# Dense block of a two-layer transformer: second weights fetched slot by slot during the projection, split rows made anew instead of kept in DRAM, the fourth block's rows turned in two parts

## The chip, the core and the metric

The kernel runs on one core of a Trainium2 chip. Its engines work from queues of their own: TensorE (PE in the profile, PEld its weight loads), VectorE (DVE), ScalarE (ACT), GpSimd (POOL) and SyncE (SP), which here issues nearly all transfers. The metric is the time of one execution on the device in microseconds; the median of the runs is compared. It was measured at 3495.49 us before the change.

## What is computed

Two equal layers, each an attention block and a dense block with a residual addition around it, on 2048 rows of 640 numbers (float32):

```python
def _A_ref(x, wqkv, wo):                     # 32 heads of 20
    q, k, v = split(x @ wqkv)
    scores = jnp.einsum("bhqd,bhkd->bhqk", q, k) * (Dh ** -0.5)
    p = _softmax(scores, axis=-1)
    o = jnp.einsum("bhqk,bhkd->bhqd", p, v)
    return heads_side_by_side(o) @ wo
def _B_ref(x, w1, b1, w2, b2):               # 640 -> 1536 -> 640
    h = relu(x @ w1 + b1)
    return (h * h) @ w2 + b2
x = x + _A_ref(_layernorm(x), A_wqkv, A_wo)  # layer one
x = x + _B_ref(_layernorm(x), B_w1, B_b1, B_w2, B_b2)
x = x + _A_ref(_layernorm(x), A_wqkv, A_wo)  # layer two
x = x + _B_ref(_layernorm(x), B_w1, B_b1, B_w2, B_b2)
```

## The kernel before

**Numbers in two halves.** A float32 matrix is held as a high and a low part (a cast to float32r by ACT, and the difference by DVE), and each product is three matmuls (high x high, high x low, low x high). A *split row tile* `xnT` is [128, 2, 512]: 128 of the 640 features, both parts, 512 rows of the sequence; five of them (`KD = 5`) hold one block of rows.

**Blocks.** The sequence is cut into four blocks of 512 rows (`NQB = 4`). After a layer's attention comes the *projection* (`add_heads`): for each block, four tiles of 128 rows, each in two halves of 320 columns, 15 matmuls per half at L361; DVE adds the residual from the PSUM bank (L1355) and the result goes to DRAM (`d_x`). After each half, 8 times a block, `side()` runs one step of other work: steps 0 to 23 of `plan` belong to the second, third and fourth quarter of the projection (8 to a quarter).

**Turning the rows.** The dense block needs normalised rows with the features on the partitions. `turn_out` does it for a block in six steps: statistics (L312, L313), normalisation (L320) and a 32 x 32 transposition on DVE (L1383) for each of four tiles, each then written to DRAM in `d_t` by four transfers of 128-byte pieces. `turn_in` reads the block back as five tiles of 256 KB, and in five more steps casts (ACT, L1398) and subtracts (DVE, L1399): the split rows.

**The dense block** (`mlp`) goes over the first half of the 1536 hidden features (`fh = 0`) for the four blocks, then over the second (`fh = 1`). For one half and one block PE makes six chains of 15 products of 512 columns (L361, by `w_1`), ACT applies relu and square (L1449, L1450), DVE and ACT form sums of the halves, and 126 products of 320 columns (L1475, by `w_2`, seven products in place of eight) follow in 14 *parts* (the first 36 products open the sums, six parts have 3 more, eight have 9). Behind each part DVE adds a PSUM bank to a row tile (L1494; in some parts also the bias, L1496). A `side()` call stands before the block (-1), after each of the six chains (0 to 5), after them (6), and after each part (7 to 20). `put(gen, ...)` names the sides at which the next steps of a generator run.

**Where things lie.** 41 slots of 512 KB (`arena`) hold weights, split rows and operands of the dense block; 12 tiles of 320 KB (`xp`) hold row tiles `x`, turned tiles `y` and hidden rows `r`. The first weights `w_1` are 15 slots (8 for the first half), the second weights `w_2` 14 slots of 480 KB for each half. A slot that is taken again waits for its last reader. PSUM has eight banks, used in turn.

**Order.** Nothing is rescheduled: each engine runs its instructions in the order in which the program's text emits them, SP's transfers too. A transfer on SP whose data or slot isn't ready holds up all behind it. Before the change all of `w_1`'s first 8 slots and 3 of `w_2` are fetched after the projection's first quarter, then 5, 4 and the last 2 after the second, the third and the fourth (`loads`). Each block's split rows are written to DRAM (`d_xn`) during the first half's block, and read back by `again` for the second half. The fourth block's rows are turned out in the first dense block, at sides -1, -1, 0, 2, 4, 5. Layer one also turns its results for the next layer's attention in the second half (`ahead`): blocks three and four of `fh = 1` read them in.

## Time and profile before

| | before |
|---|---|
| median of 3 runs | 3495.49 us (3494.67 to 3496.05) |
| the profiled execution | 3491.35 us |
| its span | 3489.6 us |
| mean granted clock of TensorE | 0.993 |
| busy share PE, DVE, ACT, POOL | 99%, 82%, 78%, 23% |
| moved by DMA | 521.39 MB, 149 GB/s over the span |

The profile is one execution. Its rows give a start in us from the span's start, a duration, the engine, the line of the program, what is written and read, and in brackets how long the engine was idle before and what ended that. A buffer's number is left out, so `xnT` is any of the split row tiles. Projection and dense block of layer one lie between about 1341 and 1754 us, those of layer two from 3079 us to the end. Lines of the program after the change are up to ten lower: L1399 is L1398, L1494 is L1493.

### The profile page before, as it was taken

What the parts mean: (1) busy time and instruction counts of PE and PEld (TensorE: products, weight loads), DVE (VectorE), ACT (ScalarE), POOL (GpSimd) and SP (SyncE); (2) the same over time, 40 slices, a digit from 0 to 9 for tenths busy, and PEclk for the clock granted to TensorE, in tenths of its full rate; (3) what the DMA queues carried; (4) which work ended last, traced back from release to release, by engine and by line L of the source; (5) the groups of instructions that cost most, each with busy time, mean ns of one, the idle gap of its engine ahead of it and who ended that gap; (6) DMA issues with size and microseconds to landing.
All of it is one profiled execution on the core that took longest, in us unless ns stands there. A gap on an engine that the chain in (4) does not pass through costs nothing. (4 is left out here: it accounts for less than half of the span.)

```text
span 3489.6 us, 70164 instructions
## 1 busy us (share of the span) xinstructions
PE 3439.0 (99%) x26202; PEld 2152.2 (62%) x26202; DVE 2850.0 (82%) x5410; ACT 2704.5 (78%) x4362; POOL 799.2 (23%) x963
## 2 busy tenths in 40 slices
PE   9999999999999999899999999999999999998999
PEld 7897444444444447799889964444444444477998
DVE  8888999999999983556768889999999999835555
ACT  3778999999999993243437799999999999923433
POOL 6531445521121121100053201221121121110000
PEclk9999999999999999899999999999999999998999
DMA  9866555422211137956687652232232111389553
GB/s 308 285 236 178 175 168 181 145 80 76 62 52 43 44 115 235 270 188 235 189 299 261 192 155 76 69 80 69 63 86 56 50 46 43 119 257 258 201 221 110
DMA packets 400325, 521.39 MB, mean 149 GB/s; under 512 B 179188, under 2 KB 226804, under 8 KB 399984
## 3 DMA queue, kind: packets, MB, share of 16 engines
q1 hardware_dynamic: 399168, 514.55, 47.1%
q8 instruction: 206, 3.38, 0.4%
q10 hardware_dynamic: 816, 2.36, 0.2%
q14 instruction: 135, 1.11, 0.1%
HBM read 304.80 MB, written 211.98 MB: 148 GB/s over the span
## 5 line engine op out<-in xcount | busy, mean ns | idle before, releaser
L561 DVE TENSOR_REDUCE mx<-banks 128x1 f32<-128x512 f32 x2096 | 1430.1, 686 | 135.4 <-PE banks L549 34.4
L549 PE MATMUL banks<-k,q 60*128 60x512 f32 (+1 forms) x4488 | 1310.6, 370 | 2.0 <-DVE v L445 2.0
L549 PEld LDWEIGHTS banks<-k,q 60*128 60x128 f32 x4488 | 715.7, 184 | 831.4 <-DVE mx L596 723.6
L684 ACT ACTIVATE e<-banks 128x512 f32<-128x512 f32 x1988 | 1192.7, 601 | 15.8 <-PE banks L676 2.2
L690 PE MATMUL banks<-e,vg 128*32 128x512 f32 x8192 | 1092.5, 605 | 1.5 <-ACT e L1295 1.5
L676 PE MATMUL banks<-q,k 62*128 62x512 f32 x3968 | 1076.6, 421 | 0.6 <-DVE mx L617 0.6
L686 ACT ACTIVATE e<-banks 128x1024 f32<-128x1024 f32 x990 | 1007.5, 1018 | 1.5
L596 DVE TENSOR_REDUCE mx<-banks 128x2 f32<-128x512 f32 x928 | 633.7, 683 | 3.3 <-PE banks L549 3.3
L676 PEld LDWEIGHTS banks<-q,k 62*128 62x128 f32 x3968 | 578.8, 184 | 53.8 <-ACT e L684 51.9
L617 DVE CUSTOM_DVE_ANT_0 rl<-banks,rl 128x512 f32<-128x512 f32 x536 | 350.2, 689 | 77.7 <-PE banks L549 58.6
L609 ACT ACTIVATE rl<-banks 128x512 f32<-128x512 f32 x538 | 295.8, 596 | 101.0 <-PE banks L549 79.0
L399 PE MATMUL banks<-xnT,wqk 64*128 64x512 f32 x2400 | 372.3, 393 | 1.8 <-DVE x L1494 1.1
L361 PE MATMUL banks<-xnT,w 128*128 128x512 f32 x1440 | 336.0, 394 | 9.9 <-DVE xnT L1399 9.9
L690 PEld LDWEIGHTS banks<-e,vg 128*32 128x32 f32 x8192 | 161.2, 108 | 259.8 <-issue 256.0
L361 PEld LDWEIGHTS banks<-xnT,w 128*128 128x128 f32 x1440 | 273.1, 190 | 68.4 <-DVE xnT L1399 12.2
L399 PEld LDWEIGHTS banks<-xnT,wqk 64*128 64x128 f32 x2400 | 296.8, 186 | 29.8 <-issue 2.0
L1475 PE MATMUL banks<-w,hs 128*128 128x320 f32 x1728 | 271.6, 316 | 20.9 <-DVE x L1494 17.2
L1475 PEld LDWEIGHTS banks<-w,hs 128*128 128x128 f32 x1728 | 262.9, 193 | 26.0 <-DVE x L1494 20.4
L1449 ACT ACTIVATE r<-banks,b_t 128x512 f32<-128x512 f32 x96 | 66.0, 688 | 256.0 <-PE banks L361 219.8
L339 POOL CAST mr<-nt 128x32 fp32r<-128x32 f32 x64 | 13.4, 210 | 1077.3 <-DVE nt L643 1077.3
L734 POOL TENSOR_TENSOR few<-few,minus_t 128x16 f32<-128x16 f32 x62 | 179.8, 2900 | 199.9 <-DMA few<-d_s 199.7
L399 PE MATMUL banks<-wv,xnT 64*128 64x320 f32 x1920 | 208.8, 307 | 0.8 <-ACT mark_t L401 0.8
(104 smaller groups left out, 2651.3 us busy)
## 6 DMA issues: line engine op xcount, KB each, us to landing
q<-d_qk SPq DMA_DIRECT2D x240, 240.0 KB
d_qk<-ev SPq DMA_DIRECT2D x80, 512.0 KB
k<-d_qk SPq DMA_DIRECT2D x152, 240.0 KB
w<-d_w SPq DMA_DIRECT2D x56, 480.0 KB
d_qk<-ev SPq DMA_DIRECT2D x80, 256.0 KB
d_xn<-xnT SPq DMA_DIRECT2D x40, 512.0 KB
xnT<-d_xn SPq DMA_DIRECT2D x40, 512.0 KB
d_o<-ot SPq DMA_DIRECT2D x248, 80.0 KB
```

Source lines behind the costliest of these rows:

```text
L361: nc.tensor.matmul(dst, a, b, start=(n == 0), stop=(n == last))
L399: m = nc.tensor.matmul(ch["dst"][:, :width], *pair, start=first, stop=last)
L549: return nc.tensor.matmul(dst, q_t[t][b : b + 60, p, sub * P : (sub + 1) * P], k_t[t // NQB, c][b : b + 60, p, keys], start=True, stop=True,)
L561: nc.vector.tensor_reduce(maxima(t)[:, 2 * par + p, sub, c : c + 1], dst, axis=AX.X, op=ALU.max)
L596: r = nc.vector.tensor_reduce(maxima(t)[:, p : p + 3 : 2, sub, c if not half else column(t, p, sub)], bank.rearrange("q (r k) -> q r k", r=2),
L609: nc.scalar.activation(res, dst, AF.Relu)
L617: nc.vector.tensor_tensor_reduce(out=r, in0=dst, in1=r, scale=1.0, scalar=LEAST, op0=ALU.add, op1=ALU.max, accum_out=maxima(t)[:, 2 * par ...
L676: nc.tensor.matmul(dst, k_t[t // NQB, kt // 4][b : b + 62, p, (kt % 4) * P : (kt % 4 + 1) * P], q_t[t][b : b + 62, p, :], start=True, stop ...
L684: nc.scalar.activation(es[h], dst, AF.Exp, scale=SCALE)
L686: nc.scalar.activation(es[pair], banks[:, 1:3, :], AF.Exp, scale=SCALE)
L690: nc.tensor.matmul(acc[32 * h : 32 * h + 32, :], v_t[t // NQB, kt // 8][:, kt % 8, 32 * h : 32 * h + 32], es[h], start=(kt == 0), stop=(kt ...
L1475: nc.tensor.matmul(dst[:, :HALF], t[:, hx, c : c + P], w_2.piece(j, p, hw), start=start and p == 0 and (hx, hw) == THREE[0], stop=stop and ...
```

## The change

Six things are altered in the text. The first 8 slots of `w_1` are fetched before the projection's first quarter. The 14 slots of `w_2` are fetched one at a time, at steps 0, 1, 3, 4, 6, 7, 9, 11, 13, 15, 17, 19, 21 and 23 of the projection's plan, and the read of the first block's rows moves from step 10 to 8. `d_xn` is gone: the split rows of the second half are made anew from `d_t` by `turn_in`, so that every block but the last of the second half now ends with a `turn_in` for its successor (read at side 6, split at 15 to 19, where the first half had 13 to 17). The fourth block's rows are turned out by three steps in the first dense block and three in the second. `d_t` gets two more buffers, since its first four are now needed to the end of the second half. And of the three blocks that are read in for the next layer, the first is split at sides 18, 19, 20, 20, 20 in place of 16 to 20, and the last is split by `second()`, within the next layer's attention.

```diff
@@ -299,10 +299,9 @@
     d_m = dram.tile([2, 2, 32, 4, 32], F32R, name="d_m")
     d_s = dram.tile([NBLK, 4, QB], F32, name="d_s")
     d_r = dram.tile([NBLK, 4, QB], F32, name="d_r")
-    d_t = [dram.tile([D, QB], F32, name=f"d_t{i}") for i in range(5)]
+    d_t = [dram.tile([D, QB], F32, name=f"d_t{i}") for i in range(7)]
     d_x = [dram.tile([S, D], F32, name=f"d_x{i}") for i in range(3)]
     d_half = dram.tile([S, D], F32, name="d_half")
-    d_xn = dram.tile([NQB, KD, P, 2, QB], F32R, name="d_xn")
 
     def stats(x):
 
@@ -1402,7 +1401,7 @@
     def new_rows():
         return [slot([P, 2, QB], F32R, "xnT") for _ in range(KD)]
 
-    rows_3 = []
+    rows_3, in_2 = [], []
 
     def to_normal(x, mv):
         y = xtile("y")
@@ -1548,16 +1547,14 @@
             return lambda i: row_tile(src, tb * 4 + i)
 
         xnt = []
-        loads = [
-            [lambda s=s: w_1.load(s) for s in range(8)] + [lambda s=s: w_2.load(0, s) for s in range(3)],
-            [lambda s=s: w_2.load(0, s) for s in range(3, 8)],
-            [lambda s=s: w_2.load(0, s) for s in range(8, 12)],
-            [],
-        ]
+        for n in range(8):
+            w_1.load(n)
         plan = [[] for _ in range(24)]
         in_0 = turn_in(d_t[0], lambda: xnt)
-        for i in (10, 14, 15, 17, 19, 21):
+        for i in (8, 14, 15, 17, 18, 20):
             plan[i].append(lambda: next(in_0))
+        for n, i in enumerate((0, 1, 3, 4, 6, 7, 9, 11, 13, 15, 17, 19, 21, 23)):
+            plan[i].append(lambda n=n: w_2.load(0, n))
         for qb in range(NQB):
             if qb + 2 == NQB:
                 xnt.extend(new_rows())
@@ -1570,14 +1567,11 @@
             if qb == 0:
                 steps.extend([None] * (24 - len(steps)))
                 steps[:] = [(lambda n=n, f=f: [f and f()] + [g() for g in plan[n]]) for n, f in enumerate(steps)]
-            for f in loads[qb]:
-                f()
             if qb + 1 == NQB:
                 all_steps()
         w_o.drop()
-        for s in range(12, w_2.n):
-            w_2.load(0, s)
-        outs = [(turn_out(d_t[3], rows), (-1, -1, 0, 2, 4, 5))]
+        out_3 = turn_out(d_t[3], rows)
+        outs = [(out_3, (-1, 0, 2)), (out_3, (-1, 0, 2))]
         rows = None
         for fh, qb in ((fh, qb) for fh in range(2) for qb in range(NQB)):
             new = []
@@ -1595,34 +1589,26 @@
 
                 return get
 
-            def again(qb):
-                new.extend(new_rows())
-                for k in range(KD):
-                    dma(nc.sync, new[k], d_xn[qb, k])
-
-            if not fh and qb + 1 < NQB:
-                put(turn_in(d_t[qb + 1], to(new)), 6, 13, 14, 15, 16, 17)
-                plan[20].append(lambda: [dma(nc.sync, d_xn[qb + 1, k], new[k]) for k in range(KD)])
-            elif (fh, qb) != (1, NQB - 1):
-                plan[7].append(lambda: again((qb + 1) % NQB))
+            if (fh, qb) != (1, NQB - 1):
+                put(turn_in(d_t[(qb + 1) % NQB], to(new)), 6, 15, 16, 17, 18, 19)
             if outs:
-                put(*outs[0][:1], *outs.pop()[1])
+                gen, at = outs.pop(0)
+                put(gen, *at)
             rows = []
             if ahead and fh and qb + 1 < NQB:
-                gen = turn_out(d_t[2 + qb], rows)
+                gen = turn_out(d_t[4 + qb], rows)
                 put(gen, 18)
                 outs.append((gen, (-1, 0, 2, 4, 5)))
-            if (fh, qb) == (0, 0):
-                plan[4].append(lambda x=list(xnt): [dma(nc.sync, d_xn[0, k], x[k]) for k in range(KD)] and x.clear())
             if not fh and qb + 1 == NQB:
                 for n in range(7):
                     plan[(0, 0, 2, 4, 4, 4, 5)[n] + 1].append(lambda n=n: w_1.load(8 + n))
             if ahead and fh and qb + 2 >= NQB:
-                for tb, at in enumerate((13, 6, 11)):
+                for tb, at in enumerate(((13, 18, 19, 20, 20, 20), (6, 11, 12, 13, 14, 15), (11,))):
                     if (tb == 0) == (qb + 2 == NQB):
                         xt_[tb] = []
-                        d = 3 if tb == 0 else 5
-                        put(turn_in(d_t[2 + tb], to(xt_[tb])), at, *[min(at + d + i, 20) for i in range(5)])
+                        gen = turn_in(d_t[4 + tb], to(xt_[tb]))
+                        put(gen, *at)
+                        in_2[:] = [gen]
             if ahead and fh and qb + 1 == NQB:
                 for n in range(5):
                     plan[11 + n].append(lambda n=n: w_qk.load(n))
@@ -1638,8 +1624,12 @@
     def second():
 
 
+        gen = in_2.pop()
         rows_3[3] = to_normal(*rows_3[3])
         yield 5.0, turns(3, rows_3, ps_q, (1, 3))
+        for _ in range(KD):
+            next(gen)
+            yield 0.7, None
 
     def constants():
 
```

How the order changes is shown at three places. The first is SP's queue at the start of layer one's projection; `w_...<-d_w_96` is a slot of the first weights, `d_w_97` of the second, `x` a row tile read for the next quarter, `d_x` one stored. Before:

```order
L76 DMA d_x_111<-x_15456 128x640
L76 DMA x_15635<-in_A_x_dram 128x640
L76 DMA d_x_111<-x_15458 128x640
L76 DMA w_15672<-d_w_96 128x1024
L76 DMA w_15674<-d_w_96 128x1024
L76 DMA w_15676<-d_w_96 128x1024
L76 DMA w_15678<-d_w_96 128x1024
L76 DMA w_15680<-d_w_96 128x1024
L76 DMA w_15682<-d_w_96 128x1024
L76 DMA w_15684<-d_w_96 128x1024
L76 DMA w_15686<-d_w_96 128x1024
L76 DMA w_15688<-d_w_97 128x960
```

After, from the last two of the eight slots on:

```order
L76 DMA w_15533<-d_w_96 128x1024
L76 DMA w_15535<-d_w_96 128x1024
L76 DMA x_15537<-in_A_x_dram 128x640
L76 DMA d_x_113<-x_15453 128x640
L76 DMA x_15574<-in_A_x_dram 128x640
L76 DMA d_x_113<-x_15455 128x640
L76 DMA x_15613<-in_A_x_dram 128x640
L76 DMA d_x_113<-x_15457 128x640
L76 DMA x_15652<-in_A_x_dram 128x640
L76 DMA d_x_113<-x_15459 128x640
L76 DMA x_15689<-in_A_x_dram 128x640
L76 DMA w_15707<-d_w_97 128x960
```

The first weights now stand ahead of the row loads of the first quarter, and the second weights no longer follow them in one go.

The second is SP's queue in the first dense block of layer one; `d_t_109<-y` writes a turned tile of the fourth block, `x<-d_x` reads a row tile to which the block adds, `d_xn<-xnT` writes the first block's split rows, `xnT<-d_t_107` reads the second block's rows. Before:

```order
L76 DMA d_t_109<-y_16331 32x20x32 x4
L76 DMA x_16400<-d_x_111 128x640
L76 DMA x_16422<-d_x_111 128x640
L76 DMA d_t_109<-y_16366 32x20x32 x4
L76 DMA x_16470<-d_x_111 128x640
L76 DMA d_xn<-xnT_15900 128x1024
L76 DMA d_xn<-xnT_15901 128x1024
L76 DMA d_xn<-xnT_15902 128x1024
L76 DMA d_xn<-xnT_15903 128x1024
L76 DMA d_xn<-xnT_15904 128x1024
L76 DMA x_16498<-d_x_111 128x640
L76 DMA d_t_109<-y_16436 32x20x32 x4
```

After:

```order
L76 DMA d_t_108<-y_16292 32x20x32 x4
L76 DMA d_x_113<-x_16063 128x640
L76 DMA x_16387<-d_x_113 128x640
L76 DMA x_16409<-d_x_113 128x640
L76 DMA d_t_109<-y_16353 32x20x32 x4
L76 DMA x_16457<-d_x_113 128x640
L76 DMA x_16480<-d_x_113 128x640
L76 DMA xnT_16514<-d_t_107 128x512
L76 DMA xnT_16515<-d_t_107 128x512
L76 DMA xnT_16516<-d_t_107 128x512
L76 DMA xnT_16517<-d_t_107 128x512
L76 DMA xnT_16518<-d_t_107 128x512
```

The five writes of split rows are gone, and of the fourth block's turned tiles one stands here in place of four.

The third is DVE's queue at the end of the third block of the second half in layer one; `x<-banks` adds a bank to a row tile, `x<-x,b_t` adds the bias, `xnT` is a split. Before:

```order
L1399 TENSOR_TENSOR xnT_18755<-xnT_18755 128x512
L1494 TENSOR_TENSOR x_18606<-banks,x_18606 128x320
L1496 TENSOR_TENSOR x_18606<-x_18606,b_t 128x640
L1399 TENSOR_TENSOR xnT_18756<-xnT_18756 128x512
L1494 TENSOR_TENSOR x_18629<-banks,x_18629 128x320
L1496 TENSOR_TENSOR x_18629<-x_18629,b_t 128x640
L312 BN_STATS bst_18824<-x_18536 128x6 x2
L313 BN_AGGR mv_18825<-bst_18824 128x2
L1399 TENSOR_TENSOR xnT_18757<-xnT_18757 128x512
L1494 TENSOR_TENSOR x_18606<-banks,x_18606 128x320
L1399 TENSOR_TENSOR xnT_18758<-xnT_18758 128x512
L1494 TENSOR_TENSOR x_18629<-banks,x_18629 128x320
```

After (`xnT_186..` are the next block's rows, made anew; `xnT_187..` those for the next layer):

```order
L1495 TENSOR_TENSOR x_18617<-x_18617,b_t 128x640
L1398 TENSOR_TENSOR xnT_18687<-xnT_18687 128x512
L1493 TENSOR_TENSOR x_18640<-banks,x_18640 128x320
L1495 TENSOR_TENSOR x_18640<-x_18640,b_t 128x640
L1398 TENSOR_TENSOR xnT_18688<-xnT_18688 128x512
L311 BN_STATS bst_18839<-x_18547 128x6 x2
L312 BN_AGGR mv_18840<-bst_18839 128x2
L1398 TENSOR_TENSOR xnT_18766<-xnT_18766 128x512
L1493 TENSOR_TENSOR x_18617<-banks,x_18617 128x320
L1398 TENSOR_TENSOR xnT_18689<-xnT_18689 128x512
L1398 TENSOR_TENSOR xnT_18767<-xnT_18767 128x512
L1493 TENSOR_TENSOR x_18640<-banks,x_18640 128x320
```

The splits for the next layer begin two parts later, and between the additions now stand those of the next block as well.

## Prediction

> **What bounds the kernel now.** I read the page's busy times first, then the list of who TensorE (PE) waited for, then PE's instructions in order of time, then the windows by stage.
>
> ```profile
> span 3489.6 us, 70164 instructions
> PE 3439.0 (99%) x26202; PEld 2152.2 (62%) x26202; DVE 2850.0 (82%) x5410; ACT 2704.5 (78%) x4362; POOL 799.2 (23%) x963
> ...
> PE banks L1475 <- DVE x L1494: 17.2, 11, 4.4
> PE banks L361 <- DVE xnT L1399: 9.9, 4, 2.9
> ```
>
> PE is busy for 99% of the span and the change leaves its instruction count as it is, so only PE's idle time and its slow time can be won. The two longest entries of its wait list (total, times, longest) belong to the dense block: it waits for VectorE (DVE) to empty a bank (L1494) or to finish a split row (L1399). The next rows show where.
>
> ```profile
> 1341.09 2.46 PE L361 MATMUL banks<-wo,ot 128*128 128x320 f32 x15
> ...
> 1412.44 2.46 PE L361 MATMUL banks<-xnT,w 128*128 128x512 f32 x10
> 1417.75 1.65 PE L361 MATMUL banks<-xnT,w 128*128 128x512 f32 x3 [2.85 <-DVE xnT L1399]
> ...
> 1475.90 20.57 PE L361 MATMUL banks<-xnT,w 128*128 128x512 f32 x90
> ...
> 1502.47 12.48 PE L1475 MATMUL banks<-w,hs 128*128 128x320 f32 x84
> 1514.79 20.59 PE L361 MATMUL banks<-xnT,w 128*128 128x512 f32 x90
> ...
> 3150.76 2.46 PE L361 MATMUL banks<-xnT,w 128*128 128x512 f32 x10
> ...
> 3213.66 20.59 PE L361 MATMUL banks<-xnT,w 128*128 128x512 f32 x90
> ```
>
> A block of the dense part is 90 products at L361 and 126 at L1475. The second block of layer one runs from 1475.90 to 1514.79, 38.9 us, with no wait: 20.4 us for the 90 (0.227 each), 18.5 for the 126 (0.147 each). The first block runs from 1412.44 to 1475.90, 63.5 us, and in layer two from 3150.76 to 3213.66, 62.9 us. **The first block of each layer loses 24.6 and 24.0 us.** The windows (length, PE busy, ... granted clock, DMA share, GB/s) say how:
>
> ```profile
> 1412.40:1475.90 63.50, 49.36 (x218) 41.59 (x217) 41.22 (x87) 17.50 (x29) 6.91 (x15) 0.84 0.91 239
> 3150.70:3213.70 63.00, 48.54 (x219) 40.91 (x218) 41.48 (x88) 17.49 (x29) 7.17 (x15) 0.84 0.91 236
> ...
> 1346.00:1361.00 15.00, 15.00 (x105) 15.00 (x104) 6.30 (x10) 0.62 (x1) 0.00 (x0) 1.00 0.59 190
> 1361.00:1377.00 16.00, 16.00 (x111) 16.00 (x111) 11.76 (x27) 0.00 (x0) 3.77 (x8) 1.00 1.00 382
> ...
> 1412.40:1434.00 21.60, 16.62 (x64) 12.78 (x63) 17.13 (x39) 3.67 (x6) 5.36 (x12) 0.84 0.99 243
> 1434.00:1451.30 17.30, 14.37 (x74) 11.77 (x72) 13.48 (x27) 10.10 (x17) 1.55 (x3) 1.00 0.95 213
> ...
> 3084.00:3099.00 15.00, 15.00 (x105) 15.00 (x104) 6.61 (x10) 0.62 (x1) 0.00 (x0) 1.00 0.58 178
> ```
>
> In the first block PE sits idle for 63.5 - 49.4 = 14.1 us, and its clock averages 0.84, which loses another 0.16 x 63.5 = 10.2: together 24.3 of the 24.6. The clock falls where PE starves (the gap of 2.85 us above), so the two go together. Behind both is DMA: its engines are 95 to 100% busy in the rows shown from 1361 to 1451, yet only 59% in the first quarter of the projection (1346 to 1361), and 58% in layer two. DVE's own waits there name the transfers (total, times, longest):
>
> ```profile
> DVE xnT L1399 <- ACT xnT L1398: 12.6, 2, 8.0
> DVE y L1383 <- DMA d_t<-y: 7.9, 2, 6.3
> DVE x L1494 <- DMA x<-d_x: 5.2, 1, 5.2
> ...
> 1406.91 0.69 DVE L1399 TENSOR_TENSOR xnT<-xnT 128x512 fp32r<-128x512 f32 x1 [8.00 <-ACT xnT L1398]
> ...
> 1420.80 0.67 DVE L1399 TENSOR_TENSOR xnT<-xnT 128x512 fp32r<-128x512 f32 x1
> ...
> 1461.29 0.89 DVE L1494 TENSOR_TENSOR x<-banks,x 128x320 f32<-128x320 f32 x2 [5.20 <-DMA x<-d_x]
> 1466.78 0.69 DVE L1399 TENSOR_TENSOR xnT<-xnT 128x512 fp32r<-128x512 f32 x1 [4.60 <-ACT xnT L1398]
> ```
>
> **The change part by part.** Prices of the transfers first, from two stretches, one of whole slots and one mostly of turned rows in 128-byte pieces:
>
> ```profile
> DMA packets 1079, 3.88 MB, mean 388 GB/s; under 512 B 128, under 2 KB 128, under 8 KB 1079
> ...
> q1 hardware_dynamic: 1079, 3.88, 100.0%
> ...
> DMA packets 4710, 1.19 MB, mean 184 GB/s; under 512 B 4466, under 2 KB 4466, under 8 KB 4709
> ...
> q1 hardware_dynamic: 4709, 1.18, 89.8%
> ...
> L1398 ACT CAST xnT<-xnT 128x512 fp32r<-128x512 f32 x35 | 20.9, 618 | 84.6 <-DMA xnT<-d_t 83.8
> ```
>
> At 388 GB/s a slot of 512 KB takes 1.35 us and one of 480 KB 1.27. The second stretch is 6.5 us long: 89.8% is 5.84 us; its 0.61 MB that are not small pieces cost 1.6, so 4466 small ones cost 4.2, and a turned tile of 2560 pieces 2.4 us.
>
> *First weights ahead of the projection, second weights a slot at a time.* Eight slots, 10.8 us of DMA, now stand before the first quarter's row loads, where 41% of 15 us, 6.2 us, was free. So everything behind is up to 6.2 us earlier (bounds 0, if slots come free late, and 6.2). The row loads of the second quarter queue behind these slots on SP: the first lands at about 1346 + 10.8 + 0.8 = 1357.6, and is wanted when the quarter's 120 products begin, 17.6 us after the start at 1341.1; PE's eight banks would cover a delay. Ahead of the loads of the first block's rows stand 6 second-weight slots in place of 8: 2.5 us more. The first load landed by 1406.9 - 0.6 (the cast) = 1406.3; now 1406.3 - 8.7 = 1397.6. Before, the fifth split began 13.9 us after the first (1406.91 to 1420.80); the same from 1398.2 puts it at 1412.1, done at 1412.8. PE needs it twelve products into the block, at 1412.4 + 2.7 = 1415.1. This wait goes, with some 2 us to spare.
>
> *Split rows made anew.* Twenty 512 KB writes per layer vanish and twenty such reads become reads of half the size. Five of the writes stood ahead of the first block's last row load: 6.8 us. *Fourth block's rows in two parts.* Three of its four tiles go to the next block; one stood ahead of that load (2.4), all three ahead of the second block's rows (7.3).
>
> Now the end of the first block. The last row load landed at 1461.3; less 6.2 + 6.8 + 2.4 it lands at 1445.9. The second block's rows were in by 1466.8 - 0.6 = 1466.2; less 6.2 + 6.8 + 7.3 they are in at 1445.9. Unhindered, PE wants the bank that waits for the last two rows when 72 of the 126 products are done: 1412.4 + 20.4 + 10.6 = 1443.4. The row before the last lands 0.8 us sooner, at 1445.1, plus an addition of 0.5: PE waits about 2.2 us. The splits now stand two parts later (first one wanted at about 1444.7, or 1447 with that slip), so no wait is added by them. With 0.8 us for what I can't see I leave **3 us** per first block: 21.6 and 21.0 us are won. Bounds: nothing left (24.6, 24.0), or all three DMA terms only half as good, which the first rival prices.
>
> *What is added: 20 casts on ScalarE (ACT) and 20 splits on DVE per layer.* A part of nine products takes 9 x 0.147 = 1.32 us of PE. DVE's rows:
>
> ```profile
> L312 DVE BATCH_NORM_STATS2 bst<-x 128x6 f32<-128x320 f32 x64 | 28.0, 479 | 0.0
> ...
> L313 DVE BATCH_NORM_AGGREGATE mv<-bst 128x2 f32<-128x12 f32 x32 | 6.7, 209 | 1.1
> ...
> L1494 DVE TENSOR_TENSOR x<-banks,x 128x320 f32<-128x320 f32 x112 | 51.6, 487 | 24.3 <-PE banks L1475 19.0 <-DMA x<-d_x 5.2
> L1399 DVE TENSOR_TENSOR xnT<-xnT 128x512 fp32r<-128x512 f32 x35 | 23.8, 680 | 15.3 <-ACT xnT L1398 15.3
> L1496 DVE TENSOR_TENSOR x<-x,b_t 128x640 f32<-128x640 f32 x16 | 13.2, 825 | 0.5
> ```
>
> An addition and a split are 1.17 us, inside a part; in the two parts that also add the bias (0.83) it is 2.0, so DVE falls 1.4 us behind, and with a row's statistics (2 x 0.48 + 0.21 = 1.2, in three blocks of layer one) 2.6. The last split then ends up to 2.6 us after the block; PE reads it 2.7 after. Cost 0; without that cover 5 x 0.68 = 3.4 us per block, in four blocks per layer, 27 us in all. ACT has nothing else at those places. On SyncE's (SP's) queue no wait is new; POOL keeps its order.
>
> *Tail of layer one.* The third block of the second half and the last one lose time to DVE:
>
> ```profile
> 1707.87 1.59 PE L1475 MATMUL banks<-w,hs 128*128 128x320 f32 x9 [1.05 <-DVE x L1494]
> ...
> 1750.01 2.90 PE L1475 MATMUL banks<-w,hs 128*128 128x320 f32 x18 [2.41 <-DVE x L1494]
> 1754.05 3.69 PE L399 MATMUL banks<-xnT,wqk 64*128 64x512 f32 x30 [1.15 <-DVE x L1494]
> ```
>
> The splits behind 1.05 wait two parts longer for their data, so about 1.6 with its aftermath goes; five splits leave the last block: one stands ahead of the addition that ends the 2.41 (0.6 off), four ahead of the one that ends the 1.15 (0.8 off, the statistics stay), 1.4 in all. Together 3.0; bounds 0 and 1.05 + 2.41 + 1.15 + 0.8 = 5.4.
>
> **Sum.** 21.6 + 21.0 + 3.0 = 45.6 us. The profiled execution took 3491.35 us (its span 3489.6), the median of the runs is 3495.49, 4.1 more. So 3445.8 for an execution like the profiled one, and **3450** for the median.
>
> **Rivals.** *Half of it stays.* DMA was busy 91% of the first block; if the early start is worth nothing (slots come free late, or row loads suffer behind the weights) the last row lands at 1452.1, PE waits 8.4 us, the clock halves again, as it did after the gap of 2.85, for about 6.8 us (in 1412.4 to 1434, 16% of 21.6 us of lost clock is 3.5, which is 6.9 us at half), so 12 stay per block: 12.5 + 12 + 3 = 27.5 won, **3468**. For it: the stage is full to the brim; against: 41% free share in both layers.
>
> *The two or three us that stay halve the clock.* 3.5 more per layer: 42.1 - 3.5 = 38.6 won, **3457**. The row for it is the 2.85 us gap. The Trainium skill, "TensorE: Matmul & The Clock Gate", Part 1, says that the clock is halved only after an idle window of about 3.4 us; by that rule my 3 us would not halve it and the time stays at 3450. The trace speaks against so firm a limit, since 2.85 us of idle was enough here.
>
> *Slower: the remade splits end too late.* One DVE queue, in order; in four blocks per layer the next block's first products wait for the fifth split. It decides once DVE is later than its 2.7 us of cover by all five splits: 3.4 us per block, and the clock halves each time (3.5): 8 x 6.9 = 55 us against 45.6, **3505**. For it: 2.6 of 2.7 us of cover used by my count in three blocks; against: the other five have no statistics in them, and DVE has idle time earlier in each block.
>
> *The change does nothing measurable*, if PE's first blocks are bound by something other than transfers, **3495**: DVE's waits for named transfers speak against.
>
> **How the numbers follow.** Chances: forecast 0.62 (3443 to 3453), halved clock 0.14, half stays 0.17, slower 0.04, nothing 0.03. The range reaches from 3441 (nothing left of the first blocks' loss, and some more of the tail: 24.6 + 24.0 + 5.4 = 54.0) to 3468; beyond lie the worse part of the second rival and the last two. A measurement of this kernel can tell about 0.2%, 7 us, from no change: faster 0.93, same 0.03, slower 0.04.
>
> **What would show each step.** The DMA share between 1346 and 1361 should be near 1. The first block of each layer should last about 42 us with the clock at 0.95 or more; no DVE wait for a split row longer than 2 us ahead of it; one wait of about 2 us at the last rows' additions. Blocks with remade splits should stay at 38.9 us. The last block of layer one should lose about 2 us in place of 4. I am wrong if the first block keeps waits of over 5 us, if DVE's transposes still wait 6 us for d_t, or if PE waits at L361 for L1399 at the start of later blocks.

## The result, and the profile after

| | before | after |
|---|---|---|
| median of 3 runs | 3495.49 us | 3454.69 us (3453.76 to 3454.87) |
| ratio | | 0.9883, 95% interval 0.986 to 0.9905 |
| the profiled execution, its span | 3491.35, 3489.6 us | 3454.69, 3452.9 us |
| first block of layer one, of layer two | 63.5, 62.9 us | 45.5, 46.3 us |
| third and last block of layer one's second half | 40.8, 42.9 us | 39.0, 42.7 us |
| moved by DMA | 521.39 MB | 489.94 MB |

The kernel is 40.8 us faster. The forecast was 3450, in a range of 3441 to 3468. The page of the kernel after shows in its first lines that the work is the same and the waits are shorter:

```profile
span 3452.9 us, 70161 instructions
PE 3425.6 (99%) x26202; PEld 2134.3 (62%) x26202; DVE 2873.9 (83%) x5450; ACT 2725.5 (79%) x4402; POOL 799.8 (23%) x963
...
L360 PE MATMUL banks<-xnT,w 128*128 128x512 f32 x1440 | 330.0, 389 | 2.5 <-DVE xnT L1398 2.5
...
L1474 PE MATMUL banks<-w,hs 128*128 128x320 f32 x1728 | 264.4, 312 | 6.0 <-DVE x L1493 2.7
```

DVE has 40 instructions more (20 splits per layer). PE's two waits have fallen, from 9.9 to 2.5 us (split rows) and from 17.2 to 2.7 us (emptied banks). PE in order of time (start, duration, in brackets the wait ahead) shows what is left of them at the places that the prediction spoke of:

```profile
1342.96 2.46 PE L360 MATMUL banks<-wo,ot 128*128 128x320 f32 x15
...
1414.31 3.14 PE L360 MATMUL banks<-xnT,w 128*128 128x512 f32 x13
1417.96 17.77 PE L360 MATMUL banks<-xnT,w 128*128 128x512 f32 x77 [0.52 <-DVE xnT L1398]
...
1439.38 3.05 PE L1474 MATMUL banks<-w,hs 128*128 128x320 f32 x19 [1.15 <-DVE hs L324]
...
1449.16 10.82 PE L1474 MATMUL banks<-w,hs 128*128 128x320 f32 x72 [0.19 <-DVE x L1493]
1459.82 20.59 PE L360 MATMUL banks<-xnT,w 128*128 128x512 f32 x90
...
3130.66 3.14 PE L360 MATMUL banks<-xnT,w 128*128 128x512 f32 x13
3135.76 17.77 PE L360 MATMUL banks<-xnT,w 128*128 128x512 f32 x77 [1.96 <-DVE xnT L1398]
...
3176.92 20.59 PE L360 MATMUL banks<-xnT,w 128*128 128x512 f32 x90
```

The first blocks run from 1414.31 to 1459.82 and from 3130.66 to 3176.92: 45.5 and 46.3 us, 17.9 and 16.6 less than before. An undisturbed block takes 38.9, so **6.6 and 7.4 us are still lost there, where the prediction left 3**. The wait for the last residual rows, 5.2 us of DVE time before, is gone from DVE's list, and PE waits 0.19 us at that bank. PE's longest wait is now for `hs` in layer one (1.15 us; an operand of the second products that DVE finishes), and for the fifth split in layer two (1.96). The windows (length, PE busy, ..., granted clock, DMA share, GB/s; the view counts a packet's whole time where it starts, so a share can come out a little over 1):

```profile
1348.00:1363.00 15.00, 15.00 (x105) 15.00 (x104) 6.16 (x10) 0.62 (x1) 0.00 (x0) 1.00 1.02 401
1414.30:1459.80 45.50, 42.00 (x218) 36.46 (x217) 34.45 (x73) 17.43 (x29) 4.77 (x10) 0.96 0.86 212
3130.70:3176.90 46.20, 42.04 (x217) 36.41 (x217) 35.72 (x76) 17.44 (x29) 4.82 (x10) 0.96 0.86 216
```

DMA is now nearly full from the projection's first quarter on (shares of 0.92 to 1.02 between 1348 and 1414). In the first block it is busy for 0.86 x 45.5 = 39.1 us, where it was 0.91 x 63.5 = 57.8 before: 18.7 us of transfers have left the block, and the block is 17.9 shorter. With shares this near to 1 a shorter block holds less DMA time whatever made it shorter, so these two numbers alone don't show the cause; but 39.1 us of transfers beside 38.9 us of products leave no slack. The list of DVE's own waits between 1343 and 1460 (total, times, longest) has one for a transfer that is long:

```profile
DVE y L1382 <- DMA d_t<-y: 12.5, 3, 8.4
```

DVE in order of time shows where it stands, and the split behind it:

```profile
1412.32 0.84 DVE L1382 STREAM_TRANSPOSE y<-x 128x640 f32<-128x640 f32 x1 [8.39 <-DMA d_t<-y]
...
1417.24 0.67 DVE L1398 TENSOR_TENSOR xnT<-xnT 128x512 fp32r<-128x512 f32 x1
...
1437.11 0.84 DVE L1382 STREAM_TRANSPOSE y<-x 128x640 f32<-128x640 f32 x1 [2.61 <-DMA d_t<-y]
```

A turned tile `y` needs one of the 12 buffers, and the one whose turn it is comes free when an earlier tile's four stores to `d_t` have landed. DVE stood 8.39 us for that ahead of the first block. Its queue is in order, so the fifth split came only at 1417.24 (PE's wait of 0.52; in layer two DVE stood 9.10 us and PE 1.96), although the first had begun at 1396. It stood 2.61 us again inside the block, with the additions that make `hs` behind it (PE's 1.15). The wait was there before (7.9 us in two pieces), and the change made it longer. The experiments ask what each edit is worth, and whether the buffers, the order of the queue or the transfers themselves are behind what is left.

### The profile page after: what moved, and what is told of

Read it like the earlier page. It is cut to its first block, busy times and chain, and to the rows that moved or that the text cites. A ratio compares the mean times of both kernels' runs of the same rounds, so it can differ in the third digit from the quotient of the medians.

```text
span 3452.9 us, 70161 instructions
## 1 busy us (share of the span) xinstructions
PE 3425.6 (99%) x26202; PEld 2134.3 (62%) x26202; DVE 2873.9 (83%) x5450; ACT 2725.5 (79%) x4402; POOL 799.8 (23%) x963
## 2 busy tenths in 40 slices
DMA packets 394566, 489.94 MB, mean 142 GB/s; under 512 B 178548, under 2 KB 226164, under 8 KB 394224
## 3 DMA queue, kind: packets, MB, share of 16 engines
q1 hardware_dynamic: 393408, 483.09, 45.5%
## 4 chain that ended last, share of the span: by engine, by line
PE 87%; DVE 1%; DMA 1%; issue 1%; SPq 1%; ACT 0%; POOL 0%; DVEq 0%; ACTq 0%; POOLq 0%
PE banks L689 29%; PE banks L548 17%; PE banks L675 14%; PE banks L360 12%; PE banks L1474 8%; PE banks L398 6%; SPq L76 1%; PE banks L1287 0%; DMA d_t<-y 0%; DVE bst L311 0%; DMA d_x<-x 0%; ACT hs L323 0%; DMA x<-in_A_x_dram 0%; DVE xnT L1398 0%; DVE y L1382 0%
## 5 line engine op out<-in xcount | busy, mean ns | idle before, releaser
L675 PEld LDWEIGHTS banks<-q,k 62*128 62x128 f32 x3968 | 579.5, 184 | 53.8 <-ACT e L683 51.9
L1474 PE MATMUL banks<-w,hs 128*128 128x320 f32 x1728 | 264.4, 312 | 6.0 <-DVE x L1493 2.7
```

The source lines that it names most:

```text
L675: nc.tensor.matmul(dst, k_t[t // NQB, kt // 4][b : b + 62, p, (kt % 4) * P : (kt % 4 + 1) * P], q_t[t][b : b + 62, p, :], start=True, stop ...
L1474: nc.tensor.matmul(dst[:, :HALF], t[:, hx, c : c + P], w_2.piece(j, p, hw), start=start and p == 0 and (hx, hw) == THREE[0], stop=stop and ...
```

## The experiments

Each kernel was timed beside the kernel before on the same chip; block lengths are those of its profiled execution, read as above. e8 and e10 leave out putting the pieces of a turned tile in their places, so what they compute is not the function; they show only what the pieces cost.

| kernel | median, us | ratio to before, 95% interval | first blocks, us |
|---|---|---|---|
| the change | 3454.69 | 0.9883 (0.986 to 0.9905) | 45.5, 46.3 |
| e1 weights' order alone | 3481.73 | 0.9955 (0.9938 to 0.9971) | 62.3, 59.5 |
| e2 all but the weights' order | 3467.79 | 0.9916 (0.9902 to 0.9931) | 52.3, 52.8 |
| e3 13 tiles | 3455.31 | 0.9879 (0.9865 to 0.9894) | 47.0, 45.6 |
| e4 second weights later | 3457.97 | 0.9887 (0.9872 to 0.9901) | 48.0, 48.6 |
| e5 fourth block all later | 3459.21 | 0.9892 (0.9877 to 0.9906) | 46.3, 46.9 |
| e6 fourth block as before | 3463.75 | 0.9908 (0.9891 to 0.9924) | 49.5, 48.5 |
| e7 split rows kept | 3464.85 | 0.9908 (0.9893 to 0.9922) | 52.2, 51.9 |
| e8 tiles stored in whole rows | 3440.44 | 0.9837 (0.9823 to 0.9852) | 38.9, 38.9 |
| e9 pieces on the load | 3461.79 | 0.9899 (0.9885 to 0.9914) | 38.9, 41.2 |
| e10 before, whole rows | 3457.97 | 0.9884 (0.9868 to 0.9901) | 47.5, 45.3 |
| e11 tail's splits back | 3454.66 | 0.9878 (0.9864 to 0.9893) | 45.9, 46.2 |
| e12 pieces on the load, dense part | 3442.72 | 0.9852 (0.9836 to 0.9869) | 40.6, 40.2 |

### What each edit is worth

**e1**, on the kernel before, takes the two changed pieces of the weights' order:

```diff
-        loads = [
-            [lambda s=s: w_1.load(s) for s in range(8)] + [lambda s=s: w_2.load(0, s) for s in range(3)],
-        ...
+        for n in range(8):
+            w_1.load(n)
 ...
-        for i in (10, 14, 15, 17, 19, 21):
+        for i in (8, 14, 15, 17, 18, 20):
             plan[i].append(lambda: next(in_0))
+        for n, i in enumerate((0, 1, 3, 4, 6, 7, 9, 11, 13, 15, 17, 19, 21, 23)):
+            plan[i].append(lambda n=n: w_2.load(0, n))
```

> The kernel before with the weight order alone: eight first-weight slots ahead of the projection, second weights a slot at a time, the first block's row loads two steps earlier; split rows still kept in DRAM, fourth block still turned in one block. Theory A (the first block of each layer is late because the DMA queue ahead of it is full, and each edit takes a piece off that queue): the gap at the block's start goes (DVE wait for xnT under 2 us), but the rows at its end still come some 9 us late; first blocks 53 to 57 us (63.5 and 62.9 before, 45.5 and 46.3 with the whole change), time 3476 to 3484 us. Rival B (the order of the weights is the whole gain): first blocks 45 to 48, time 3455 to 3462. Rival C (the bytes saved are the whole gain): first blocks 61 to 63, time over 3488.

The first blocks are 62.3 and 59.5 us: 1.2 and 3.4 won, far less than the 6 to 10 of Theory A, though the time lies in its range. The rows of DVE in layer one tell why:

```profile
1416.91 0.84 DVE L1383 STREAM_TRANSPOSE y<-x 128x640 f32<-128x640 f32 x1 [8.49 <-DMA d_t<-y]
...
1462.12 0.89 DVE L1494 TENSOR_TENSOR x<-banks,x 128x320 f32<-128x320 f32 x2 [5.11 <-DMA x<-d_x]
```

The wait of 8.0 us for the first block's rows is gone, but the wait for a tile's buffer, 1.58 us at this transposition before, is 8.49 now: one took the other's place. And the last residual rows were used 47.5 us after the block's start (1462.12 against 1414.65), 48.9 before: 1.4 us sooner, not 6.2. By medians e1 wins 15 us, by the blocks 4.6; its profiled execution was the longest of its four (3485.43) and that of before under all its timed runs, so where the other ten lie isn't settled.

**e2** is the rest of the change, with the weights as before (the edit of e1 undone in the changed kernel).

> The changed kernel with the weights in the old order (eight first and three second slots after the first quarter, then bursts of 5, 4 and 2), all else as changed. Theory A: the gap at the block's start stays (a DVE wait for xnT of 6 to 9 us ahead of it, PE gap about 3 us), the rows at the end come 9 us sooner than before; first blocks 52 to 56, time 3473 to 3481. Its gain and that of the weight order alone add up to 35 to 45 us. Rival B: first blocks 61 to 63, time over 3488. Rival C: first blocks 45 to 48, time 3455 to 3462.

The blocks are as Theory A had them, 52.3 and 52.8 us; the time, 3467.8 us, is 5 us below its range. DVE waits 9.57 us for the first split, and PE 3.22 at the block's start:

```profile
1410.16 0.69 DVE L1398 TENSOR_TENSOR xnT<-xnT 128x512 fp32r<-128x512 f32 x1 [9.57 <-ACT xnT L1397]
...
1420.65 1.65 PE L360 MATMUL banks<-xnT,w 128*128 128x512 f32 x3 [3.22 <-DVE xnT L1398]
```

So the weights' order is worth 6.8 and 6.5 us per first block on top of the other edits, and 1.2 and 3.4 without them. The edits help each other: by e1's rows, a transfer that comes sooner is worth something only if the next thing in the queue doesn't hold up the same engine.

**e6 and e7** undo one of the other two edits each:

```diff
 e6
-        out_3 = turn_out(d_t[3], rows)
-        outs = [(out_3, (-1, 0, 2)), (out_3, (-1, 0, 2))]
+        outs = [(turn_out(d_t[3], rows), (-1, -1, 0, 2, 4, 5))]
 e7
 ...
-            if (fh, qb) != (1, NQB - 1):
-                put(turn_in(d_t[(qb + 1) % NQB], to(new)), 6, 15, 16, 17, 18, 19)
+            if not fh and qb + 1 < NQB:
+                put(turn_in(d_t[qb + 1], to(new)), 6, 15, 16, 17, 18, 19)
+                plan[20].append(lambda: [dma(nc.sync, d_xn[qb + 1, k], new[k]) for k in range(KD)])
+            elif (fh, qb) != (1, NQB - 1):
+                plan[7].append(lambda: again((qb + 1) % NQB))
 ...
```

> The changed kernel with the fourth block's rows turned in one go in the first block, as before (sides -1, -1, 0, 2, 4, 5). Theory E: two tiles' stores more in the first block, one of them (about 2.4 us) ahead of its last row load and DVE waits again: first blocks 47 to 51 us, time 3458 to 3466. Rival H (the split in two parts does nothing, the other two edits are the gain): first blocks 45 to 47, time 3453 to 3457.

> The changed kernel with the split rows kept in DRAM and read back as before (40 transfers of 512 KB per layer), instead of made anew; weights and fourth block as changed. Theory E: five writes of 512 KB, 6.8 us of DMA, stand again ahead of the first block's last row loads: first blocks 50 to 53 us, later blocks 38.9 in place of 38.97, time 3463 to 3470. Rival H2 (these writes fit beside the rest): first blocks 45 to 47, time 3453 to 3457.

Both fell where Theory E had them. The fourth block in two parts is worth 4.0 and 2.3 us per first block (49.5 and 48.5 against 45.5 and 46.3), the rows made anew 6.7 and 5.6 (52.2 and 51.9). In e7 the blocks that hold remade splits in the changed kernel take 38.90 in place of 38.97 (one of them 39.2, by a wait): the remade splits cost 0.07 each.

### What is left of the first block's loss

**e3** gives the pool one more buffer, 13 for 12 (`NX = 13`).

> The changed kernel with 13 in place of 12 tiles in the pool that holds residual rows, turned rows and activations. Theory D (what is left of the first blocks' loss is DVE standing for a turned tile's buffer, which is given back by the stores of an earlier block's tile): the 8.4 us wait at L1382 ahead of the first block falls under 4 us, the one of 2.6 in it goes, first blocks 42 to 44 us, time 3447 to 3452. Rival E (the transfers themselves are late, the buffer only shows it): the waits move to other rows, first blocks 45 to 47, time 3453 to 3457.

Theory D fell. The long wait is 8.1 us and stands one tile earlier, before the stage's eighth transposition in place of the ninth. The one inside the block has gone to ACT, which needs a buffer of the same pool for its hidden rows, and PE waits behind it (DVE's row, then ACT's, then PE's):

```profile
1405.69 0.84 DVE L1382 STREAM_TRANSPOSE y<-x 128x640 f32<-128x640 f32 x1 [8.14 <-DMA d_t<-y]
...
1437.02 0.69 ACT L1448 ACTIVATE r<-banks,b_t 128x512 f32<-128x512 f32 x1 [4.64 <-DMA d_t<-y]
...
1439.07 0.56 PE L1474 MATMUL banks<-w,hs 128*128 128x320 f32 x2 [2.02 <-ACT hs L323]
```

**e4** moves three slots of the second weights behind the stores that DVE waited for:

```diff
-        for n, i in enumerate((0, 1, 3, 4, 6, 7, 9, 11, 13, 15, 17, 19, 21, 23)):
+        for n, i in enumerate((0, 1, 3, 4, 6, 7, 15, 16, 17, 18, 19, 21, 22, 23)):
```

> The changed kernel with the slots of the second weights that stood at steps 9, 11 and 13 moved behind the stores of the second block's first turned tiles (steps 0, 1, 3, 4, 6, 7, 15, 16, 17, 18, 19, 21, 22, 23 in all). Theory D: those stores leave up to 4 us sooner, the 8.4 us wait at L1382 falls to 3 to 6 us, first blocks 43 to 45, time 3449 to 3453. Rival E (the queue is full, and the order only decides who waits): first blocks 45 to 47, time 3453 to 3457. Rival F, slower: eight slots now stand among the last steps, PE waits for second weights at L1474, first blocks 47 to 51, time 3457 to 3465.

The last wait ahead of the block fell to 3.65 us, as Theory D expected, and PE starts the block without a gap. But the one ahead of it rose from 1.50 to 4.66 us, so DVE's waits there went only from 9.9 to 8.3 together. The wait inside the block rose from 2.61 to 6.26, and the block takes 48.0 us, 2.5 more than after the change. The later stores now stand behind the weights in the queue, which fits this:

```profile
1393.75 0.85 DVE L1382 STREAM_TRANSPOSE y<-x 128x640 f32<-128x640 f32 x1 [4.66 <-DMA d_t<-y]
...
1408.68 0.84 DVE L1382 STREAM_TRANSPOSE y<-x 128x640 f32<-128x640 f32 x1 [3.65 <-DMA d_t<-y]
...
1438.58 0.85 DVE L1382 STREAM_TRANSPOSE y<-x 128x640 f32<-128x640 f32 x1 [6.26 <-DMA d_t<-y]
...
1440.85 4.58 PE L1474 MATMUL banks<-w,hs 128*128 128x320 f32 x19 [4.49 <-DVE hs L324]
```

The time is in Rival F's range for another reason than F's: PE didn't wait for weights.

**e5** takes the fourth block's rows out of the first block altogether: `outs = [(out_3, ()), (out_3, (-1, 0, 1, 2, 4, 5))]`.

> The changed kernel with the fourth block's rows turned wholly in the second block (sides -1, 0, 1, 2, 4, 5), none of it in the first. Theory E (what is left of the first blocks' loss is the turned tiles' stores on a full DMA queue; the tile buffers only decide which engine is seen waiting): two tiles' stores fewer in the first block, the waits on hs at L1474 shrink, first blocks 42 to 44.5 us, time 3448 to 3452. Rival G (four row tiles are now held through the first block, so the 12 buffers run out and the waits only move): first blocks 45 to 49, time 3454 to 3462.

Rival G: 46.3 and 46.9 us, and the second block rises to 40.2. The four row tiles now stay in the pool through the block, and ACT waits 5.07 us for a buffer. From e3 to e5, neither one buffer more nor another order shortened both first blocks; they decided which engine is seen waiting.

**e8** leaves queue and buffers alone and changes what a store costs. The transfers are as many and as large, but go out in rows of 2560 bytes in place of 128-byte pieces:

```diff
-                t0 = i * P + 32 * a
+                r0 = i * 160 + 40 * a
 ...
-                    d[:, t0 : t0 + 32].rearrange("(b j) t -> j b t", j=32),
-                    y[32 * a : 32 * a + 32].rearrange("j (b t) -> j b t", t=32),
+                    d[r0 : r0 + 40].rearrange("r t -> (r t)").rearrange("(j f) -> j f", j=32),
+                    y[32 * a : 32 * a + 32],
```

> The changed kernel with the turned tiles stored in rows of 2560 bytes instead of pieces of 128 bytes: as many stores and bytes, but the pieces of a tile are not put in their places, so the values that follow are others. Theory E: a tile's stores take about 0.9 us of DMA in place of 2.4, the queue drains, DVE's waits at L1382 fall under 2 us in all and the first blocks come to 39 to 41.5 us, time 3440 to 3447. Rival I (bytes, not pieces, fill the queue, or the wait is the fixed latency of a store): first blocks 44 to 46.5, time 3452 to 3456.

**The whole loss goes.** PE in order of time has no wait between the start of the first block and that of the second:

```profile
1412.82 20.59 PE L360 MATMUL banks<-xnT,w 128*128 128x512 f32 x90
...
1451.73 20.59 PE L360 MATMUL banks<-xnT,w 128*128 128x512 f32 x90
```

DVE's list of waits between 1341 and 1452 has 0.3 us left for a tile's buffer:

```profile
DVE y L1382 <- DMA d_t<-y: 0.3, 1, 0.3
```

And the windows of the two first blocks have DMA busy for about half the time:

```profile
1412.80:1451.70 38.90, 38.90 (x218) 35.37 (x217) 27.06 (x57) 17.05 (x29) 2.76 (x6) 1.00 0.54 179
3121.50:3160.40 38.90, 38.90 (x218) 35.36 (x218) 26.99 (x57) 17.06 (x29) 2.75 (x6) 1.00 0.47 154
```

How many pieces fall into the first block of layer one is in the view of DMA over that stretch, the count "under 512 B"; before:

```profile
DMA packets 33215, 15.18 MB, mean 239 GB/s; under 512 B 29344, under 2 KB 29344, under 8 KB 33212
```

after:

```profile
DMA packets 21184, 9.67 MB, mean 212 GB/s; under 512 B 18494, under 2 KB 18494, under 8 KB 21182
```

and e8:

```profile
DMA packets 3262, 6.95 MB, mean 179 GB/s; under 512 B 573, under 2 KB 573, under 8 KB 3260
```

The prediction's price for a piece (4.2 us for 4466, 0.94 ns) makes 18494 - 573 pieces 16.9 us. The DMA time of the block fell from 39.1 to 0.54 x 38.9 = 21.0, by 18.1. The two are near each other, but not the same thing: with the queue emptier, transfers also end before the block begins (16 stores to `d_t` of 80 KB are under way in it in place of 25, and 2 slots of second weights in place of 5). A tile has 2560 pieces: without the 573 others, about 11 tiles' worth went out within the first block before, 7 after. Over the whole kernel e8 spares 112640 pieces, by that price 106 us of DMA time, and wins 14 us: most of the pieces cost the kernel nothing.

**e10** makes the same edit in the kernel before.

> The kernel before with the turned tiles stored in rows of 2560 bytes, as in e8 (the pieces are not put in their places): Theory E, taken to its end (the 128-byte pieces are what fills the queue, and every edit of the change only makes room for them): the kernel before loses little without them, first blocks 39 to 43 us, time 3446 to 3456. Rival L (the old order of the weights and the kept rows hurt by themselves): first blocks 48 to 56, time 3465 to 3482.

Neither: 47.5 and 45.3 us. Without the pieces the first blocks are 16.0 and 17.6 us shorter than before, but they still lose 8.6 and 6.4: a wait for the first block's rows stays (10.14 us of DVE time, 1.54 of PE at the block's start), and the second block's rows come late (ACT waits 5.36 us for them). So the old order costs time by itself too. e10 is as fast as the changed kernel (ratio 0.9884 to 0.9883): the change and the cheaper stores are two ways to empty the same queue, and together (e8) they win 56 us.

### A faster version

**e9** stores a tile as it stands, and puts the pieces in place when they are read:

```diff
-    d_t = [dram.tile([D, QB], F32, name=f"d_t{i}") for i in range(7)]
+    d_t = [dram.tile([QB, D], F32, name=f"d_t{i}") for i in range(7)]
 ...
+            dma(nc.sync, d[i * P : (i + 1) * P, :], y)
 ...
-            dma(nc.sync, res[k][:, 1, :], d[k * P : (k + 1) * P, :])
+            for b in range(4):
+                dma(
+                    nc.sync,
+                    res[k][32 * b : 32 * b + 32, 1, :].rearrange("j (a t) -> j a t", t=32),
+                    d[:, (4 * k + b) * 32 : (4 * k + b + 1) * 32].rearrange("(a j) t -> j a t", j=32),
+                )
```

> The changed kernel with the layout of the turned tiles in DRAM changed: a tile is stored as it stands (one store in rows of 2560 bytes), and the 128-byte pieces are put in place by the loads, four for each split row. Theory E: up to the end of the first block 14 tiles are stored and two blocks (8 tiles) are loaded, so pieces for 6 tiles fewer, 6 x 1.5 = 9 us of DMA less: DVE's waits at L1382 go, first blocks 40 to 44 us, time 3443 to 3450. Rival K (the pieces now stand right ahead of the splits that PE waits for): a wait for xnT of 3 us or more comes back at the start of the first block, or in later blocks, time 3455 to 3470.

Each came true in part. The first blocks are 38.9 and 41.2 us, as good as Theory E had them or better, but the time is Rival K's, and lies in other places than a wait of PE for `xnT`: layer one's last block is 50.2, and the time from there to the projection of layer two rose from 1323.1 to 1333.9. ACT's casts show the loads' rate, and PE's row at the change of layers what they hold up:

```profile
1692.35 0.62 ACT L1396 CAST xnT<-xnT 128x512 fp32r<-128x512 f32 x1 [1.43 <-DMA xnT<-d_t]
...
1694.50 0.62 ACT L1396 CAST xnT<-xnT 128x512 fp32r<-128x512 f32 x1 [1.53 <-DMA xnT<-d_t]
...
1745.41 9.61 PE L398 MATMUL banks<-xnT,wqk 64*128 64x512 f32 x59 [7.16 <-DMA wqk<-d_wqk]
```

**e12** therefore keeps the old layout for the tiles that layer one turns ahead (`[QB, D] if i < 4 else [D, QB]`, and both forms in the two functions).

> The changed kernel with the layout of e9 (whole rows stored, pieces put in place by the loads) for the four blocks' tiles of the dense part alone; the tiles that layer one turns ahead for layer two keep the old layout. Theory E: the first blocks are as in e9 (38.9 and 41.2 us in place of 45.5 and 46.3), and the last block of layer one and the change of layers are as in the changed kernel again, since what e9 lost lay there (its last block 50.2 us in place of 42.7): 6.6 + 5.1 = 11.7 us less than 3454.7, so 3441 to 3446. Rival K (loads in pieces cost time in the other blocks too): 3447 to 3458.

3442.7 us (3441.0 to 3444.8), 12 less than the change and within what was expected. All its runs are faster than all runs of the change, though the intervals of the two ratios overlap by a little (0.986 to 0.9869). The view of DMA over the first block of layer one, and its window:

```profile
DMA packets 13266, 8.06 MB, mean 198 GB/s; under 512 B 10868, under 2 KB 10868, under 8 KB 13263
```

```profile
1411.80:1452.50 40.70, 39.25 (x219) 35.45 (x218) 32.81 (x69) 16.94 (x29) 4.63 (x10) 1.00 0.64 198
```

10868 pieces are left of 18494, DMA has a third of the block free, and PE has one wait of 1.45 us left. DVE still stands for a tile's buffer ahead of the block, but this time PE doesn't wait behind it:

```profile
1408.29 0.84 DVE L1385 STREAM_TRANSPOSE y<-x 128x640 f32<-128x640 f32 x1 [6.83 <-DMA d_t<-y]
```

Layer one's last block takes 45.2 us, 2.5 more than after the change: ACT stands 2.54 and 2.37 us for loads in pieces at its start, and PE waits for `hs` (0.59 and 0.77 us), which it didn't after the change. That is Rival K in one block; that the loads cause all of the 2.5 us was not tested. By the table the blocks make 4.9 + 6.1 - 2.5 = 8.5 of the 12 us; the rest lies outside them, and its cause is open. Over the whole kernel e12 moves more small pieces than the change, 262772 packets under 512 bytes against 178548, since each block is read for both halves.

### The tail of layer one

**e11** puts the five splits that are made ahead in the third block back to sides 16 to 20.

> The changed kernel with the five splits made ahead in the third block of layer one's second half at sides 16 to 20, as before, in place of 18, 19, 20, 20, 20. Theory J (those splits, two parts later, put DVE behind at the start of the last block, whose new wait of 1.50 us eats what its own missing splits gave): the last block falls from 42.7 to 40.8 to 41.6 us, the third one rises from 38.96 by up to 1.8. Rival M (the last block's waits come from its statistics and normalised rows): last block 42.4 to 42.9. Time 3453 to 3457 by both, so the blocks decide.

The third block rises to 39.9 and the last falls to 42.2, less than Theory J had. The rows of the last block's end, first after the change, then in e11:

```profile
1723.71 8.18 PE L1474 MATMUL banks<-w,hs 128*128 128x320 f32 x54 [1.50 <-DVE x L1493]
1732.69 2.90 PE L1474 MATMUL banks<-w,hs 128*128 128x320 f32 x18 [0.81 <-DVE x L1493]
```

```profile
1723.58 8.18 PE L1474 MATMUL banks<-w,hs 128*128 128x320 f32 x54 [0.52 <-DVE x L1493]
1733.30 2.90 PE L1474 MATMUL banks<-w,hs 128*128 128x320 f32 x18 [1.54 <-DVE x L1493]
```

The wait of 1.50 that is new with the change does come from the later splits (it falls to 0.52), but the later wait grows from 0.81 to 1.54 in its place. Where DVE's splits stand shifts the wait and doesn't remove it. DVE is busy for 36.9 of the last block's 42.7 us, so it may simply have too much to do there; no run shows it.

## Why the prediction was right, and where a size was off

**The bound: right.** The loss of the first blocks came from a full DMA queue: it vanished in e8, where only the form of the stores was changed, and leaving out any one edit (e2, e6, e7) brought part of it back. e10 adds that the old order loses 8.6 and 6.4 us even without the pieces.

**Weights ahead of the projection: right in the whole, not by itself.** DMA's share between 1348 and 1363 went to 1.02, as forecast near 1. The term of 6.2 us is near the 6.8 and 6.5 us that e2 lacks, but in part by luck: the clock of e2's first block is 0.93 against 0.96, so some 1.8 of the 6.8 us (0.07 x 52.3 less 0.04 x 45.5) are clock, which the term doesn't hold. "Everything behind is up to 6.2 us earlier" is not true without the other edits: alone it was 1.4 us at the last rows.

**Split rows made anew: right.** 6.8 forecast, 6.7 and 5.6 measured by e7. The remade splits cost 0.07 us a block where I put 0, far from the 3.4 of the slower rival.

**Fourth block in two parts: right in kind.** 2.4 forecast for the first block's last rows, 4.0 and 2.3 measured by e6 on the block.

**What is left of the first blocks: mis-sized.** I left 3 us each; 6.6 and 7.4 are left. That is 8.0 of the 8.9 us between the sum (3445.8 for an execution like the profiled one) and the profiled 3454.69. The step that failed is "this wait goes, with some 2 us to spare". I followed the transfers that PE's operands wait for, the rows in and the residual rows, and these did come in time (0.19 us of waiting for the last ones, where I put 2.2). I didn't follow the stores of the turned tiles, whose buffers DVE needs, through the new order of the queue, though the view of before had the row (7.9 us, the longest 6.3). A sign that the prediction itself named for being wrong appeared: DVE's transpositions still wait more than 6 us for `d_t`, 8.39 and 9.10. e8 shows the amount: without the pieces' price the blocks lose nothing. e3, e4 and e5 show that neither a buffer more, nor another order, nor a later turn of the fourth block sets it right.

**The clock: partly.** The rival in which the small rest halves the clock happened in part: 0.96 in both first blocks, 0.04 x 45.5 = 1.8 us each, half of the 3.5 that it was priced at. With 45.5 - 42.0 = 3.5 us of idle time that names 5.3 of the 6.6 us; the rest is in the view's busy time.

**The tail: 3.0 forecast, 2.0 measured.** The third block gave 1.8 of 1.6; the last 0.2 of 1.4. Its two old waits fell from 2.41 and 1.15 to 0.81 and 0.58, more than forecast, but a new one of 1.50 came ahead of them, from the splits that the change moves to the third block's end (e11).

**The step from profile to median** went the other way: the profiled execution of before lay 4.1 us under its median, that of after at its median. So medians fell by 40.8 us, profiled executions by 36.7, with 45.6 forecast. That the median came within 5 us of 3450 is partly luck: nearly half of the sum's miss of 8.9 us was made up by the 4.1 us added for this step, which the kernel after doesn't show. 3454.69 lies just outside the band of 3443 to 3453 given to the forecast itself, between it and the 3457 of the rival with the halved clock.

## What to carry to other kernels

When transfers fill a stretch, count what each adds to the queue in time and not in bytes (here a turned tile of 320 KB takes 2.4 us, as much as 930 KB of whole slots at 388 GB/s), and then follow every engine that waits for a buffer given back by one of them, not only those that wait for data. An edit that frees such a queue is worth its price only once the other waits on the same engine are gone as well, so edits of this kind have to be measured in the whole and by leaving out one, not one at a time. Before reordering a full queue, look for the transfer whose form makes it dear: on top of the change, moving the small pieces to stretches with free DMA time (e12) won 12 us, where one buffer more and other orders (e3 to e5) won nothing.

## What the runs showed of the hardware

**Half clock without a long gap.** After the change PE was idle in short waits from 1438 to 1446, the longest 1.15 us, and ran at half clock from 1445.5 to 1449.0, for about 3.4 us (windows of PE: length, busy, clock, DMA share, GB/s):

```profile
1442.00:1444.00 2.00, 1.27 (x7) 1.00 0.81 191
1444.00:1446.00 2.00, 1.09 (x7) 0.88 1.02 241
1446.00:1447.00 1.00, 1.00 (x4) 0.50 1.16 153
...
1449.00:1450.00 1.00, 0.84 (x6) 1.00 1.07 290
```

With 13 tiles, in layer one, a wait of 2.02 us at the same place, followed by a like series of short ones, left the clock at 1.00 throughout:

```profile
1434.00:1440.00 6.00, 3.67 (x22) 1.00 1.05 194
1440.00:1446.00 6.00, 4.67 (x27) 1.00 1.01 228
1446.00:1452.00 6.00, 4.19 (x27) 1.00 0.88 316
```

In layer two of the same run the clock did halve, for 3.4 us, though no wait in the 10 us ahead was longer than 0.74 us. Before the change, the stretch behind the gap of 2.85 us lasted 6.8 us, from 1417.8 to 1424.6. So neither the longest wait nor the idle time of some microseconds decides alone. The Trainium skill, "TensorE: Matmul & The Clock Gate", Part 1, gives a free-running window of about 3.4 us and one idle window as the condition. The lengths of the half-clock stretches, 3.4 us and twice that, agree with such a window, and so does it that a longer wait elsewhere left the clock alone. That the window must be idle does not agree: PE was busy for 2.07 of the 3.40 us ahead of the fall (1442.1 to 1445.5), and no wait there came near 3.4 us.

**A small piece costs about as much on a load as on a store.** In e9 the casts at 1692.35 and 1694.50 wait for loads in pieces, one split row tile (2048 pieces) apart. In the 2.15 us between them nothing but pieces moved (the window, then the view of DMA over it):

```profile
1692.35:1694.50 2.15, 2.15 (x12) 1.76 (x11) 0.69 (x1) 0.62 (x1) 0.00 (x0) 1.00 0.81 127
...
DMA packets 2192, 0.27 MB, mean 127 GB/s; under 512 B 2192, under 2 KB 2192, under 8 KB 2192
```

A share of 0.81 makes 1.74 us of DMA time, 0.79 ns a piece; the stores of before came to 0.94 ns by the prediction's price, which is DMA time too.
